# Attention and two gated layers on one core: the width in which ScalarE stores the scaled lower words of the weights

## The chip, the cores and the metric

The kernel runs on one core of one Trainium2 chip. The metric is the device time of one execution in microseconds (us), given as the median of several runs. Besides the time of each run there is one profiled execution of the kernel before, whose trace is quoted below.

## The reference

Windowed attention (4 batches, 8 heads, 576 positions, window of 64) feeds two gated layers in a row. Each layer multiplies 2304 tokens of width 512 with two weight matrices of 512 x 1536, gates one product by a function of the other, and multiplies the result with a third matrix of 1536 x 512.

```python
scores = scale * np.matmul(q, k.transpose(0, 1, 3, 2))       # then masked, softmax
x = np.matmul(attn, v)                                       # -> (2304, 512)
g = x @ w_gate; silu = g * (1.0 / (1.0 + np.exp(-g)))
x = (silu * (x @ w_val)) @ w_out                             # layer 1
...
gate = 1.0 / (1.0 + np.exp(-(x @ w_gate)))
out = (gate * (x @ w_val)) @ w_out                           # layer 2
```

Every one of the six weight matrices arrives as 64-bit floating point numbers, so it has to be turned into 32-bit numbers on the chip before TensorE can use it.

## The kernel before, in words

The tokens are cut into five tiles of 512, 384, 512, 512 and 384 tokens. For each layer and each tile the kernel walks over 12 slices of the hidden width; a slice has three steps: the product with the gate weights (tile `g`, function `product`), the product with the value weights (`v`), and one slice later the product with the output weights (`a`, function `out_product`). Each product is done as three matmul passes over numbers split into a high and a low part: `split_hi` on ScalarE writes the high part of a weight, `split_lo` on VectorE subtracts it. The order of the work on every engine is written out by hand: the string `START` gives the order of the first stretch (attention of the first four blocks of 128 tokens, and the first six weight conversions), and dictionaries of steps (`before`, `during`, `after`) attach all other work to a step of the products. Each engine takes its instructions in that order.

The conversion of one 128x512 piece of weights is in `round_a` and `round_b`. There are 72 such pieces, 36 for each layer. A piece lands in a tile `raw` with two 32-bit words for each number, a lower and an upper one, so the words of one kind stand 8 bytes apart. In `round_a`, ScalarE does two instructions: line 377 reads the lower words as unsigned integers, scales them so that only their top three bits remain as a number, and stores it; line 380 reads the upper words, takes the absolute value and writes it contiguously into a tile `t`. In `round_b`, VectorE does four: line 388 reads the top 16 bits of the upper word (`fourth`), keeps the sign, sets one more bit and stores that into the top half of the lower word (`second`); line 389 limits `t`, line 390 shifts it left by three, and line 391 adds the lower word to it, the sum being the 32-bit number. `conv_b` and `raw_ahead` then issue the next load of a `raw` tile, of which there are four. The converted output weights of layer 1 and all weights of layer 2 are also written to memory, to be loaded again for later tiles.

The conversions of layer 1 run before and during the first token tile of layer 1, those of layer 2 during its third and fourth. In the first stretch, `x_hi` (line 328) on ScalarE and `x_lo` (line 331) on VectorE bring a block's attention result into the tile `x`, which the products read; `evacuate` (line 211) brings transposed queries out for the scores, `evacuate_p` (line 308) transposed probabilities for the product with the values (`pv`, line 318).

Of the kernel before, what the change touches and what calls it, by code (L numbers as in the profile page):

```python
# [11 lines left out]
UINT32 = mybir.dt.uint32  # L12
UINT16 = mybir.dt.uint16
ACTF = mybir.ActivationFunctionType
# [25 lines left out]
def attention_moe_moe(  # L40
# [28 lines left out]
    scale = 1.0 / float(D) ** 0.5  # L69
# [269 lines left out]
    raws = {}  # L339
# [22 lines left out]
    def words_of(r):  # L362
        w = r.rearrange("p (f two) -> p f two", two=2)
        half = r.bitcast(UINT16).rearrange("p (f four) -> p f four", four=4)
        return w[:, :, 0], w[:, :, 1], half[:, :, 0], half[:, :, 1], half[:, :, 3]

# [3 lines left out]
    def round_a(key):  # L372
        t = t_p.tile([128, 512], INT32, tag="t", name="t")
        mids[key] = t
        if wide:
            lower, upper, first, _, _ = words_of(raws[key])
            nc.scalar.activation(  # L377
                out=first, in_=lower.bitcast(UINT32), func=ACTF.Copy, scale=2.0 ** -29
            )
            nc.scalar.activation(out=t.bitcast(FP32), in_=upper.bitcast(FP32), func=ACTF.Abs)  # L380

    def round_b(key, keep):
        r = raws.pop(key)
        t = mids[key]
        tf = t.bitcast(FP32)
        if wide:
            lower, _, _, second, fourth = words_of(r)
            nc.vector.tensor_scalar(second, fourth, 0x8000, 0x4000, ALU.bitwise_and, ALU.bitwise_or)  # L388
            nc.vector.tensor_scalar(tf, tf, F64_LEAST, F64_MOST, ALU.max, ALU.min)  # L389
            nc.vector.tensor_scalar(t, t, 3, None, ALU.logical_shift_left)  # L390
            nc.vector.tensor_tensor(out=t, in0=t, in1=lower, op=ALU.add)  # L391
        else:
            nc.vector.tensor_copy(tf, r)
        mids[key] = tf
        if keep:
            d = dram.tile([128, 512], FP32, name=f"k{key[0]}{key[1]}{key[2]}")
            nc.sync.dma_start(out=d, in_=tf)
            kept[key] = d
# [117 lines left out]
    for b in range(B):  # L516
# [4 lines left out]
        first = {1: 12, 2: 24, 3: 46}[b]  # L521
# [29 lines left out]
    def conv_b(j):  # L551
        round_b(convs[j][1], convs[j][1][1] == "o")
        raw_ahead(j + 1 + 4)

    for j, (s, key) in enumerate(convs[SPLIT_EARLY:], SPLIT_EARLY):
        at(during, s + 1, round_a, key)
        at(during, s + 2, round_b, key, key[0] == 1 or key[1] == "o")
        at(during, s + 2, raw_ahead, j + 1 + 4)
        if key[0] == 0:
            plan_split(s + 2, key)  # L560
# [32 lines left out]
    for t in range(NTL, 2 * NTL):  # L593
        for fc in range(FC):
            n, key = SPT * t + 3 * fc + 5, (1, "o", fc)
# [29 lines left out]
    with tc.manual_schedule():  # L625
# [13 lines left out]
        for step in LOADS.split():  # L639
# [31 lines left out]
            "lo": lambda i: x_lo(i, x_of(0), i * 128),  # L671
            "wm": lambda k: warm(k),
            "ca": lambda j: round_a(convs[j][1]),
            "cb": lambda j: conv_b(j),
            "ch": lambda j: split_hi(convs[j][1]),
# [9 lines left out]
        for T in range(2 * NTL):  # L685
# [3 lines left out]
            for fc in range(FC):  # L689
# [7 lines left out]
                    out=s, in_=gps[:, 0:n], func=(ACTF.Silu, ACTF.Sigmoid)[m]  # L697
# [54 lines left out]
```

## Time and profile before

| | |
|---|---|
| median of 3 runs | 1010.43 us (1010.13 to 1010.93) |
| profiled execution, its own time | 1010.98 us |
| span in its trace | 1009.2 us |
| TensorE matmul busy (PE) | 984.6 us, 98% of the span |
| VectorE busy (DVE) | 516.4 us, 51% |
| ScalarE busy (ACT) | 496.7 us, 49% |
| line 377, all 72 instructions | 98.0 us |

The span is the time from the first to the last instruction in the trace; 1.78 us of the profiled execution lie around it. PE, DVE, ACT and SP stand for TensorE, VectorE, ScalarE and the engine that issues most of the DMAs. Shares of busy time are averages over the whole span, while the stretches of the kernel differ: ScalarE and VectorE are nearly full in the first 155 us and mostly idle after 500 us.

### The profile page before, as it was taken

Reading aid. Unit: us, or ns where it says so; the run is one execution under the profiler, and the core shown is the slowest. Engines: PE = TensorE matmul, PEld = TensorE weight load, DVE = VectorE, ACT = ScalarE, POOL = GpSimd, SP = SyncE. Lnnn points to the kernel's source line nnn. Section 1 sums busy time; section 2 is a strip of 40 time slices with the busy share of each in tenths; the row PEclk is TensorE's granted clock in tenths of the full one; section 3 lists DMA queues with packets and bytes.
Section 4 is the critical chain, followed back from the end, with each engine's and each line's share of the span. In section 5 each row is a group of like instructions: output and inputs, shape, how many; then the busy total and the mean of one; then the engine's idle time right before and its main releaser. Section 6 shows DMA issues by size and latency. Waiting matters only on the chain.

```text
span 1009.2 us, 14684 instructions
## 1 busy us (share of the span) xinstructions
PE 984.6 (98%) x5621; PEld 847.7 (84%) x5621; DVE 516.4 (51%) x1181; ACT 496.7 (49%) x981; POOL 4.1 (0%) x20
## 2 busy tenths in 40 slices
PE   8899998999999999999999999999999999999998
PEld 6677777999878788888999888899988888888997
DVE  6899994554576777767555323223322222223322
ACT  6899994655676668657444322222222222222222
POOL 1000000000000000000000000000000000000000
PEclk7799999999999999999999999999999999999999
DMA  9647798773176666573644400020020002000100
GB/s 225 187 152 214 205 234 205 196 151 108 55 223 204 203 201 223 172 233 106 210 146 146 167 1 1 1 84 1 1 73 1 1 1 73 0 1 1 42 1 32
DMA packets 164982, 113.03 MB, mean 112 GB/s; under 512 B 102704, under 2 KB 139568, under 8 KB 164912
## 3 DMA queue, kind: packets, MB, share of 16 engines
q1 hardware_dynamic: 161264, 111.18, 38.1%
q10 hardware_dynamic: 3648, 0.92, 0.4%
q8 instruction: 44, 0.72, 0.3%
q14 instruction: 26, 0.21, 0.1%
HBM read 90.05 MB, written 27.53 MB: 117 GB/s over the span
## 4 chain that ended last, share of the span: by engine, by line
PE 80%; DVE 7%; ACT 7%; issue 3%; SPq 2%; DMA 1%; DVEq 0%; ACTq 0%
PE a L441 26%; PE g L429 26%; PE v L429 24%; ACT raw L377 2%; SPq L118 2%; ACT z L279 1%; DVE raw L388 1%; PE att L244 1%; PE att L318 1%; DVE t L390 1%; PE att L302 1%; DMA ks<-in_k_dram 1%; ACT L279 1%; DVE t L389 1%; DVE s L705 1%
## 5 line engine op out<-in xcount | busy, mean ns | idle before, releaser
L429 PE MATMUL g<-x,wg 128*128 128x512 f32 (+1 forms) x1440 | 319.5, 370 | 0.7 <-ACT x L328 0.7
L429 PE MATMUL v<-x,wv 128*128 128x512 f32 (+1 forms) x1440 | 317.6, 369 | 0.0
L429 PEld LDWEIGHTS g<-x,wg 128*128 128x128 f32 x1440 | 264.6, 189 | 38.0 <-ACT x L328 0.9
L429 PEld LDWEIGHTS v<-x,wv 128*128 128x128 f32 x1440 | 261.2, 188 | 33.0
L705 DVE TENSOR_TENSOR s<-s,v 128x512 f32<-128x512 f32 (+1 forms) x120 | 75.9, 632 | 314.7 <-PE v L429 303.6
L696 ACT ACTIVATE s<-g 128x512 f32<-128x512 f32 (+1 forms) x120 | 66.7, 556 | 304.1 <-PE g L429 303.6
L441 PE MATMUL a<-h,wo 128*128 128x512 f32 (+1 forms) x720 | 164.8, 377 | 6.3 <-DVE h L621 6.3
L441 PE MATMUL a<-wo,h 128*128 128x512 f32 x648 | 157.4, 390 | 0.0
L707 ACT ACTIVATE h<-s 128x512 fp32r<-128x512 f32 (+1 forms) x120 | 70.6, 588 | 169.4 <-DVE s L705 169.3
L441 PEld LDWEIGHTS a<-h,wo 128*128 128x128 f32 x720 | 131.2, 190 | 26.5 <-DVE h L621 7.6
L441 PEld LDWEIGHTS a<-wo,h 128*128 128x128 f32 x648 | 121.3, 188 | 24.2
L377 ACT ACTIVATE raw<-raw 128x512 uint16<-128x512 uint32 x72 | 98.0, 1361 | 0.0
L621 DVE TENSOR_TENSOR h<-s,h 128x512 fp32r<-128x512 f32 (+1 forms) x120 | 76.2, 635 | 3.2
L388 DVE TENSOR_SCALAR raw<-raw 128x512 uint16<-128x512 uint16 x72 | 53.9, 748 | 17.4 <-ACT raw L377 17.3
L279 ACT ACTIVATE z<-z,nm 128x128 f32<-128x128 f32 x144 | 55.8, 390 | 2.8 <-DVE nm L263 2.7
L101 DVE TENSOR_TENSOR x<-rx,x 128x512 fp32r<-128x512 f32 (+1 forms) x20 | 12.8, 639 | 84.3 <-ACT x L100 84.3
L391 DVE CUSTOM_DVE_ANT_0 t<-raw,t 128x1024 uint16<-128x1024 uint16 x72 | 49.9, 693 | 2.5
L380 ACT ACTIVATE t<-raw 128x512 f32<-128x512 f32 x72 | 51.1, 710 | 0.0
L415 DVE TENSOR_TENSOR wo<-stay,wo 128x512 fp32r<-128x512 f32 x60 | 41.1, 685 | 0.0
L411 ACT ACTIVATE wo<-stay 128x512 fp32r<-128x512 f32 x60 | 37.4, 623 | 0.0
L415 DVE TENSOR_TENSOR wo<-tw,wo 128x512 fp32r<-128x512 f32 x48 | 32.9, 686 | 5.7 <-ACT wo L411 5.7
L389 DVE TENSOR_SCALAR t<-t 128x512 f32<-128x512 f32 x72 | 33.3, 462 | 0.0
(84 smaller groups left out, 569.4 us busy)
## 6 DMA issues: line engine op xcount, KB each, us to landing
raw<-in_moe_w_gate_dram SPq DMA_DIRECT2D x24, 512.0 KB, 4.2
raw<-in_moe_w_val_dram SPq DMA_DIRECT2D x24, 512.0 KB, 4.3
raw<-in_moe_w_out_dram SPq DMA_DIRECT2D x24, 512.0 KB, 3.7
tw<-k0o SPq DMA_DIRECT2D x48, 256.0 KB, 4.2
v<-in_v_dram SPq DMA_DIRECT2D x29, 256.0 KB, 4.6
out_dram<-o SPq DMA_DIRECT2D x18, 256.0 KB, 2.3
k<-ks SPq DMA_DIRECT2D x10, 384.0 KB, 5.4
k0o<-t SPq DMA_DIRECT2D x12, 256.0 KB, 2.3
```

Of the source, the lines that this page charges most:

```text
L279: nc.scalar.activation(out=z[:, hp, :], in_=z[:, hp, :], func=ACTF.Exp, scale=-1.0, bias=nm[:, hp:hp + 1], accum_out=su[:, hp:hp + 1],)
L377: nc.scalar.activation(out=first, in_=lower.bitcast(UINT32), func=ACTF.Copy, scale=2.0 ** -29)
L380: nc.scalar.activation(out=t.bitcast(FP32), in_=upper.bitcast(FP32), func=ACTF.Abs)
L388: nc.vector.tensor_scalar(second, fourth, 0x8000, 0x4000, ALU.bitwise_and, ALU.bitwise_or)
L391: nc.vector.tensor_tensor(out=t, in0=t, in1=lower, op=ALU.add)
L415: nc.vector.tensor_tensor(out=w[:, 1], in0=mids.pop(key), in1=w[:, 0].bitcast(FP32), op=ALU.subtract)
L429: nc.tensor.matmul(out=ps[:, 0:n], lhsT=w[:, a, c, :], rhs=xt[:, b, c, 0:n], start=(j == 0), stop=(j == len(mm) - 1),)
L441: nc.tensor.matmul(out=acc[e][:, 0:n] if m == 0 else acc[e], lhsT=w[:, a, cols] if m == 0 else h[:, a, cols], rhs=h[:, b, 0:n] if m == 0 e ...
L621: nc.vector.tensor_tensor(out=h[:, 1, 0:n], in0=s, in1=h[:, 0, 0:n].bitcast(FP32), op=ALU.subtract)
L696: nc.scalar.activation(out=s, in_=gps[:, 0:n], func=(ACTF.Silu, ACTF.Sigmoid)[m])
L705: nc.vector.tensor_tensor(out=s, in0=s, in1=vps[:, 0:n], op=ALU.mult)
L707: nc.scalar.activation(out=h[:, 0, 0:n], in_=s, func=ACTF.Copy)
```

## The change

The store of line 377 goes to the whole lower word as a 32-bit integer, where it went to the lower half of that word as a 16-bit integer. The upper half, which was left alone before, is now written too; VectorE's line 388 overwrites it afterwards as it did before. No instruction is added, removed or moved on any engine or DMA queue, and no instruction waits for another kind of event than before.

```diff
     def words_of(r):
         w = r.rearrange("p (f two) -> p f two", two=2)
         half = r.bitcast(UINT16).rearrange("p (f four) -> p f four", four=4)
-        return w[:, :, 0], w[:, :, 1], half[:, :, 0], half[:, :, 1], half[:, :, 3]
+        return w[:, :, 0], w[:, :, 1], half[:, :, 1], half[:, :, 3]
...
         if wide:
-            lower, upper, first, _, _ = words_of(raws[key])
+            lower, upper, _, _ = words_of(raws[key])
             nc.scalar.activation(
-                out=first, in_=lower.bitcast(UINT32), func=ACTF.Copy, scale=2.0 ** -29
+                out=lower, in_=lower.bitcast(UINT32), func=ACTF.Copy, scale=2.0 ** -29
             )
...
         if wide:
-            lower, _, _, second, fourth = words_of(r)
+            lower, _, second, fourth = words_of(r)
```

## Rows read from the trace of the kernel before

**Rows 1.** The page, part 1: busy time, share and instructions of each engine.
```profile
PE 984.6 (98%) x5621; PEld 847.7 (84%) x5621; DVE 516.4 (51%) x1181; ACT 496.7 (49%) x981; POOL 4.1 (0%) x20
```

**Rows 2.** Busy time by stretch: length, PE, PEld, DVE, ACT, POOL; clock, DMA, GB/s.
```profile
8.00:43.50 35.50, 29.00 (x307) 23.32 (x303) 30.00 (x118) 31.93 (x95) 0.00 (x0) 0.66 0.88 210
...
51.80:155.00 103.20, 93.47 (x550) 74.38 (x546) 99.58 (x232) 97.30 (x173) 0.00 (x0) 0.98 0.74 206
...
200.00:500.00 300.00, 298.25 (x1939) 254.16 (x1938) 198.24 (x490) 194.78 (x392) 0.00 (x0) 1.00 0.58 175
```

**Rows 3.** Groups of ScalarE's instructions by line and shape (busy us, mean ns).
```profile
L377 ACT ACTIVATE raw<-raw 128x512 uint16<-128x512 uint32 x72 | 98.0, 1361 | 0.0
...
L380 ACT ACTIVATE t<-raw 128x512 f32<-128x512 f32 x72 | 51.1, 710 | 0.0
...
L411 ACT ACTIVATE wg<-t 128x512 fp32r<-128x512 f32 x12 | 7.5, 623 | 1.8 <-DVE t L391 1.8
```

**Rows 4.** Timeline of 36 to 44 us: start, duration, instruction, [idle before <-releaser].
```profile
35.62 1.36 ACT L377 ACTIVATE raw<-raw 128x512 uint16<-128x512 uint32 x1
...
36.70 0.73 ACT L380 ACTIVATE t<-raw 128x512 f32<-128x512 f32 x1
...
37.33 0.59 ACT L308 ACTIVATE pt<-a 128x512 f32<-128x512 f32 x1
...
37.80 1.34 ACT L377 ACTIVATE raw<-raw 128x512 uint16<-128x512 uint32 x1
...
39.48 0.59 ACT L328 ACTIVATE x<-a 128x512 fp32r<-128x512 f32 x1
...
40.10 0.69 DVE L331 TENSOR_TENSOR x<-a,x 128x512 fp32r<-128x512 f32 x1 [0.68 <-ACT x L328]
...
40.71 0.75 DVE L388 TENSOR_SCALAR raw<-raw 128x512 uint16<-128x512 uint16 x1
...
40.85 1.98 PE L318 MATMUL a<-pt,v 128*64 128x64 f32 x32 [2.75 <-DVE x L331]
...
41.24 0.47 DVE L389 TENSOR_SCALAR t<-t 128x512 f32<-128x512 f32 x1
...
43.52 0.80 PE L429 MATMUL g<-x,wg 128*128 128x512 f32 x1 [0.70 <-ACT x L328]
```

**Rows 5.** Timeline of 20.4 to 29 us.
```profile
21.88 1.35 ACT L377 ACTIVATE raw<-raw 128x512 uint16<-128x512 uint32 x1
...
24.07 1.36 ACT L377 ACTIVATE raw<-raw 128x512 uint16<-128x512 uint32 x1
...
26.41 1.33 PE L244 MATMUL v<-kt,early_q 64*64 64x128 f32 x10 [0.66 <-ACT early_q L211]
```

**Rows 6.** All waits of VectorE, 50 to 156 us (us in total, times, longest).
```profile
DVE s L705 <- PE v L429: 2.5, 1, 2.5
DVE x L331 <- ACT x L328: 1.2, 2, 0.6
```

**Rows 7.** Waits of TensorE from 156 us to the end.
```profile
PE att L302 <- DVE z L294: 0.9, 2, 0.6
...
PE att L244 <- DVE kt L231: 0.8, 2, 0.5
```

**Rows 8.** Waits of VectorE, 260 to 484 us.
```profile
DVE raw L388 <- ACT raw L377: 15.5, 12, 1.8
```

**Rows 9.** Waits of TensorE, 8 to 156 us.
```profile
PE a L441 <- DVE h L621: 6.3, 3, 2.1
```

**Rows 10.** Stretches around the first products, columns as in Rows 2.
```profile
40.00:41.00 1.00, 0.15 (x2) 0.15 (x4) 0.90 (x2) 1.00 (x4) 0.00 (x0) 0.51 0.28 98
...
46.00:47.00 1.00, 1.00 (x5) 0.77 (x4) 1.00 (x3) 0.66 (x2) 0.00 (x0) 0.58 0.91 309
```

**Rows 11.** Stretches after two of the waits of Rows 9, same columns.
```profile
113.00:114.00 1.00, 1.00 (x5) 0.82 (x5) 1.00 (x3) 1.00 (x3) 0.00 (x0) 1.00 0.90 291
...
156.00:157.00 1.00, 1.00 (x4) 0.77 (x4) 0.78 (x2) 0.79 (x2) 0.00 (x0) 0.53 0.80 209
```

## The prediction, made before the changed kernel ran

> **What bounds the kernel now.** I read the table of engines first: TensorE is busy for 98% of the span [rows 1], so an engine that gets faster elsewhere can only give back what TensorE loses by waiting. The stretches say where that is. From 200 to 500 us TensorE is busy for 298.25 of 300 us, although half of all conversions lie there. From 8 to 43.5 us and from 51.8 to 155 us it is idle for 6.5 and 9.7 us [rows 2]. In the second of these the reader is to see two nearly full engines: VectorE busy for 99.58 of 103.20 us, ScalarE for 97.30. The waits say which of the two is the bound. In 106 us VectorE waits three times in all, 3.7 us, and once the first tile's work has begun only twice for 0.6 us each, both in line 331 for line 328 [rows 6]. TensorE meanwhile waits three times for VectorE's low half of the hidden values, 6.3 us [rows 9]. So the first tile runs at VectorE's pace, with ScalarE close behind; before it the small pieces of the start follow each other from engine to engine; after it TensorE sets the pace. The time of line 377, 98 us in 72 instructions [rows 3], must not be read as time to be gained.
>
> **The price of the new store.** Line 377 takes 1361 ns. Its neighbour, line 380, reads words 8 bytes apart of the same tile and writes them contiguously in 710 ns, and a contiguous copy of the same size takes 623 ns [rows 3]. So reading every second word costs some 90 ns, and about 650 ns of line 377 must come from its 16-bit store with gaps, from the integer formats or from working in place. No row has a 32-bit store with gaps. The timeline shows more than the mean: after line 377 starts at 35.62, line 380 starts at 36.70, 1.08 us later, while line 377 is recorded until 36.98, so 0.28 us overlap. Line 380 holds the engine for 0.63 us and overlaps its follower by 0.10 us [rows 4]. When the next instruction starts to read, line 377 still has a longer backlog to write than others. That speaks for the store, rather than for reading or converting, as the slow end. Against it: VectorE's line 388 also stores 16 bits every 8 bytes and lets its follower start after 0.53 us [rows 4], so such a store is not slow on every engine. The bounds for a 32-bit store with gaps are the contiguous copy, 623 ns, and the row of line 377 itself, 1361 ns; twice its excess over the copy is the far end of the slower rival below. I take 710 ns, since the other side of the same tile, in the same 8-byte steps and whole words, is the nearest row. That frees 0.65 us of latency and 1.08 - 0.63 = 0.45 us of ScalarE's time for each conversion, 32 us in all 72.
>
> A rule speaks against that. The rows show 1361 ns for 2-byte stores in 8-byte steps and 710 ns for 4-byte reads in the same steps [rows 3]. The Trainium skill, page "SBUF — State Buffer", section "Specifications (TRN2)", has lines of 16 bytes and wants two hits in a line for full bandwidth. By that rule both stores hit each line twice, the width would change nothing, and the sum would be zero; no row before shows whether it holds for ScalarE's stores, and the 1361 ns sit badly with it. What it would give is the second rival.
>
> **What of it reaches the end.** No instruction moves, and the wait of line 388 for line 377 stays. So the change is a shorter instruction, and what counts is where ScalarE is waited for.
>
> At the start, six conversions lie before the first product. Two stand ahead of the copy of queries that the scores at 26.41 wait for, at 21.88 and 24.07; TensorE is idle for 0.66 us there [rows 5]. Two savings of 0.45 us are more than that, so the gain is 0.66 us. Two more stand at 35.62 and 37.80, ahead of line 328 at 39.48; line 331 waits for it for 0.68 us, TensorE waits for line 331 until 40.85, and the first product starts at 43.52 behind that [rows 4]. Two savings again exceed the 0.68 us, after which VectorE's own work is the limit. Together 0.66 + 0.68 = 1.3 us.
>
> In the first tile 28 conversions give ScalarE 28 x 0.45 = 12.6 us of room, but VectorE has only its two waits, 1.2 us, to give up [rows 6]. This is the cover that makes the rest worth nothing: VectorE's own 99.6 us of work [rows 2], of which the change touches none. If VectorE did not bind, TensorE's 9.7 idle us would be the limit. What is late next is VectorE.
>
> Later, 36 conversions run behind a full TensorE. VectorE waits 15.5 us for line 377 there [rows 8], but TensorE's own waits after 156 us that these can feed are 0.9 us for line 294 and 0.8 us for line 231 [rows 7], two each. Line 377 ending 0.65 us earlier removes a wait as long as the larger, if it stands behind it on VectorE; I count half, 0.8 us.
>
> The sum is 1.3 + 1.2 + 0.8 = 3.3 us off a profiled execution of 1010.98 us (span 1009.2 and 1.78 around it), 1007.7 us; that execution was 0.55 us above the median of 1010.43, so the median goes to **1007.1 us**.
>
> **Rivals.**
> *The clock stays up at the start.* TensorE idles for 2.75 us before 40.85 and then runs at half clock, 0.51 in 40 to 41 and still 0.58 in 46 to 47 [rows 4, 10]. The idle stretch would shrink to about 2.1 us. The three later waits of 2.1 us [rows 9] went both ways: the clock was full after one and 0.53 after another [rows 11]. If it holds here, some 6 us at half clock become 3, and the time is 1007.1 - 3 = 1004 us.
>
> *The store's price stays.* For it: a 16-bit store on VectorE that keeps pace, and integer formats that stay the same. Against it: the backlog. Then nothing moves: 1010.4 us.
>
> *The price falls half-way*, to about 1.03 us. The 0.23 us saved for each conversion give 0.46 at each place of the start, 0.9 in all, about 1.0 in the first tile and 0.5 later: 1008.0 us.
>
> *The price falls and the clock takes it back.* If a wait of TensorE such as that at 113 to 114 is met with half clock near 155 us, where TensorE takes over the pace, 3 us at half clock cost 1.5 us: 1008.6 us. Earlier in the first tile VectorE's pace would cover it.
>
> *Slower:* the price goes with the bytes stored. The excess over the contiguous copy, 1361 - 623 = 738 ns, would double. ScalarE's idle time in the first tile is 103.2 - 97.3 = 5.9 us [rows 2], 0.21 us for each of 28 conversions; from that increase on ScalarE is the bound in place of VectorE. At 0.74 us it is 28 x 0.74 - 5.9 = 14.8 us there and 4 x 0.74 = 3 us at the start: 1028 us. Nothing in the rows speaks for it but that whole words are twice the bytes, and line 380, which reads as many in the same steps quickly, speaks against.
>
> **How the numbers follow.** Chances: my forecast 0.45, with a range of its own of 1005 to 1009 us (none of the later waits but all of the start and the tile, or the start half only, up; all 1.7 us of the later waits and some clock, down); the clock stays up 0.08; half-way 0.10; price unchanged 0.25; taken back by the clock 0.06; slower 0.06. About 0.2%, 2.0 us, is what a measurement of this kernel can tell from no change, so faster means below 1008.4 us. That holds for most of the forecast, for the kept clock and for a part of the half-way case: 0.54. Unchanged price, the give-back and the rest of these make 0.37 for the same; slower 0.09. The range, 1003.8 to 1011.2 us, takes in the kept clock and the unchanged price with their scatter, and leaves out the slower rival and rarer sums of good luck.
>
> **What the changed profile would show.** If the price step is right, line 377 has a mean near 710 ns and the next instruction starts about 0.6 us after it, with an overlap of 0.1 us. If the start is right, the first product begins near 42.2 us, with no wait of line 331 near 39 us. If the bound is right, VectorE stays 99 to 100 us busy in the first tile while ScalarE gains some 13 us of idle time, most of it waiting for line 705, and TensorE goes on waiting for line 621. If the later step is right, TensorE's waits for lines 231 and 294 after 156 us shrink, and VectorE's wait of 15.5 us for line 377 halves. The prediction is wrong if the mean of line 377 stays above 1.2 us, if VectorE's instructions change in length, since its pace carries the first tile, or if the granted clock falls in other places than before.

## The result, and the profile after

The changed kernel takes 1001.19 us in the median of four runs (1000.38 to 1004.74), against 1010.28 us before. The ratio is 0.9916 with a 95% interval of 0.9891 to 0.9942. Measured again with more runs of the kernel before beside it, it took 1001.23 us, ratio 0.9898 (0.9884 to 0.9913). So the gain is 9 to 10 us, where 3.3 us were forecast, and the time lies below the stated range.

The page of the changed kernel, part 1, shows ScalarE with some 40 us less work and the other engines as they were [rows 1].

```profile
PE 980.4 (98%) x5621; PEld 844.7 (84%) x5621; DVE 515.6 (52%) x1181; ACT 457.0 (46%) x981; POOL 4.1 (0%) x20
```

The groups of ScalarE's instructions by shape (busy us, mean ns) show where it went. Line 377 fell from 1361 to 666 ns [rows 3].

```profile
L380 ACT ACTIVATE t<-raw 128x512 f32<-128x512 f32 x72 | 47.9, 666 | 0.0
L377 ACT ACTIVATE raw<-raw 128x512 int32<-128x512 uint32 x72 | 47.9, 666 | 0.0
```

The timeline of the last part of the start, in the changed kernel, answers to [rows 4]. The second instruction now follows 0.57 us after line 377 starts, and the overlap is 0.14 us. Line 331 no longer waits for line 328; TensorE waits for it for 1.32 us in place of 2.75, and runs the product of line 318 in 1.15 us in place of 1.98.

```profile
35.85 0.71 ACT L377 ACTIVATE raw<-raw 128x512 int32<-128x512 uint32 x1
...
36.42 0.69 ACT L380 ACTIVATE t<-raw 128x512 f32<-128x512 f32 x1
...
36.99 0.61 ACT L328 ACTIVATE x<-a 128x512 fp32r<-128x512 f32 x1
...
38.06 0.68 DVE L331 TENSOR_TENSOR x<-a,x 128x512 fp32r<-128x512 f32 x1
...
38.80 1.15 PE L318 MATMUL a<-pt,v 128*64 128x64 f32 x32 [1.32 <-DVE x L331]
...
40.65 0.74 PE L429 MATMUL g<-x,wg 128*128 128x512 f32 x2 [0.70 <-ACT x L328]
```

The same stretches as in [rows 10] have the full clock now (the column behind POOL).

```profile
40.00:41.00 1.00, 0.35 (x2) 0.31 (x3) 0.97 (x3) 1.00 (x2) 0.00 (x0) 1.00 0.88 360
46.00:47.00 1.00, 1.00 (x6) 0.75 (x4) 0.55 (x1) 1.00 (x4) 0.00 (x0) 1.00 0.88 273
```

In the first tile ScalarE is busy for 78.02 of 94.10 us, VectorE for 91.88.

```profile
47.40:141.50 94.10, 89.50 (x525) 71.95 (x526) 91.88 (x217) 78.02 (x166) 0.00 (x0) 0.96 0.74 205
```

Of TensorE's waits after 156 us, one is left, which the kernel before has too; the two of [rows 7] are gone.

```profile
PE att L202 <- DVE x L331: 0.8, 1, 0.8
```

To see where the time came from, I compare the start of a few instructions in the two traces. The columns are the first product, then the 1st, 10th, 13th, 25th and 48th of the 120 instructions of line 705 (VectorE's product of gate and value), and the span. The first row has the times of the kernel before; the others show how much earlier (-) or later (+) each kernel's one profiled execution is. Rows with a name in e are the experiments below.

```
                   product   1st    10th    13th    25th    48th     span
before               43.52  51.79  146.25  176.53  266.81  480.74  1009.18
after                -2.88  -4.37   -5.82   -6.04   -6.09   -8.98    -8.98
e5_after_again       -3.34  -3.00   -4.49   -4.78   -4.82   -7.77    -7.62
e2_start_only        -4.49  -6.03   -5.14   -5.16   -5.20   -5.13    -5.13
e3_tile_only         -1.11  -0.78   -2.19   -0.92   -0.63   -0.55    -0.55
e4_layer2_only       -1.45  -0.14   +0.35   -0.93   -0.62   -3.52    -3.51
e6_before_warm       -1.56  -3.10   -2.31   -2.35   -2.04   -2.03    -2.03
e7_after_h_first     -3.18  -4.71   -6.17   -7.20   -7.19  -10.08   -10.07
e8_before_no389      +0.29  +0.43   -2.61   -3.31   -2.99   -2.96    -2.96
e10_after_no389      -4.93  -6.46  -18.81  -15.67  -14.73  -17.61   -17.60
```

In the changed kernel three stretches gain: 4.4 us up to line 705's first instruction, 1.4 us in the first tile (1st to 10th), and 2.9 us between the 25th and the 48th, where the second layer's weights are converted. The forecast had 1.3, 1.2 and 0.8 us.

### The profile page after: what moved, and what is told of

It is laid out like the page before. It is cut to its first block, busy times and chain, and to the rows that moved or that the text cites. A ratio compares the mean times of both kernels' runs of the same rounds, so it can differ in the third digit from the quotient of the medians.

```text
span 1000.2 us, 14684 instructions
## 1 busy us (share of the span) xinstructions
PE 980.4 (98%) x5621; PEld 844.7 (84%) x5621; DVE 515.6 (52%) x1181; ACT 457.0 (46%) x981; POOL 4.1 (0%) x20
## 4 chain that ended last, share of the span: by engine, by line
PE 86%; DVE 9%; issue 2%; DMA 1%; ACT 1%; SPq 0%; DVEq 0%
PE a L441 28%; PE g L429 27%; PE v L429 27%; DVE raw L388 2%; PE att L318 1%; DVE t L390 1%; PE att L244 1%; PE att L302 1%; DVE t L391 1%; DVE t L389 1%; DVE z L263 1%; DVE h L621 1%; DVE s L705 1%; DMA raw<-in_moe_w_val_dram 1%; DVE wv L415 0%
## 5 line engine op out<-in xcount | busy, mean ns | idle before, releaser
L391 DVE CUSTOM_DVE_ANT_0 t<-raw,t 128x1024 uint16<-128x1024 uint16 x72 | 49.8, 692 | 2.5
L380 ACT ACTIVATE t<-raw 128x512 f32<-128x512 f32 x72 | 47.9, 666 | 0.0
L377 ACT ACTIVATE raw<-raw 128x512 int32<-128x512 uint32 x72 | 47.9, 666 | 0.0
```

Of the source, the lines that this page charges most:

```text
L377: nc.scalar.activation(out=lower, in_=lower.bitcast(UINT32), func=ACTF.Copy, scale=2.0 ** -29)
```

## The experiments

### What makes the store slow

In the first kernel the second layer's 36 pieces store the scaled words in eight forms by turns, each on a line of its own (here in words):

```diff
-    nc.scalar.activation(out=lower, in_=word, func=Copy, scale=2.0 ** -29)
+    L383: out = 16-bit integers every 8 bytes in raw     L385: out = lower (32-bit integers every 8 bytes)
+    L387: out = 512 packed 16-bit integers in t          L389: out = 16-bit integers every 4 bytes in t
+    L391: out = bf16 every 8 bytes in raw                L393: out = lower as 32-bit floats
+    L395: out = 256 16-bit integers every 8 bytes in t   L397: out = 32-bit integers, packed, in t
```

> The first layer's pieces are converted as in the changed kernel; the 36 pieces of the second layer store the scaled lower words in eight forms by turns, of which only two give the right weights. Theory (half of a 32-bit word is the slow thing): 16-bit integers every 8 bytes near 1.36 us, bf16 every 8 bytes the same, 16-bit integers every 4 bytes over 1 us, half as many 16-bit integers every 8 bytes into another tile near 0.78 us; 32-bit integers and 32-bit floats every 8 bytes 0.67 us; packed 16-bit integers and packed 32-bit integers near 0.62 us. Rival A (the integer formats): bf16 every 8 bytes takes 0.67 us. Rival B (working in place): 16-bit integers into another tile run at 0.62 us for 512 and 0.42 us for 256. Rival C (gaps of any kind): the 16-bit form every 4 bytes is faster than that every 8 bytes, and 32-bit stores with gaps are slower than packed ones by as much.

The groups by shape, with the mean in ns behind the busy time:

```profile
L385 ACT ACTIVATE raw<-raw 128x512 int32<-128x512 uint32 x40 | 26.8, 670 | 0.0
...
L391 ACT ACTIVATE raw<-raw 128x512 bf16<-128x512 uint32 x5 | 6.8, 1354 | 0.0
L383 ACT ACTIVATE raw<-raw 128x512 uint16<-128x512 uint32 x4 | 5.4, 1360 | 0.0
...
L395 ACT ACTIVATE t<-raw 128x256 uint16<-128x256 uint32 x5 | 3.9, 771 | 0.0
L393 ACT ACTIVATE raw<-raw 128x512 f32<-128x512 uint32 x5 | 3.3, 662 | 0.0
L397 ACT ACTIVATE t<-raw 128x512 int32<-128x512 uint32 x5 | 3.3, 655 | 0.3 <-DVE wo L433 0.3
...
L389 ACT ACTIVATE t<-raw 128x512 uint16<-128x512 uint32 x4 | 3.1, 783 | 0.0
L387 ACT ACTIVATE t<-raw 128x512 uint16<-128x512 uint32 x4 | 2.6, 650 | 0.0
```

A bf16 store is as slow as one of 16-bit integers, so the integer formats are not it (rival A falls). A store into another tile is as slow for each element, so working in place is not it (rival B falls). Gaps alone are not it either: 32-bit words every 8 bytes take 670 ns, packed ones 655. Half words are slow only where they leave gaps, and there I missed: every 4 bytes they take 783 ns, not over 1 us. So 512 of them over 2 KB cost as much as 256 over 2 KB. A second kernel of the same kind separates the two ways to read that, called theory A and theory B in its expectation, with stores in 16- and 32-byte steps, 256 packed half words (L391) and single bytes every 8 bytes (L393):

```diff
+    L385: 256 16-bit integers every 16 bytes    L387: 128 16-bit integers every 32 bytes
+    L389: 256 32-bit integers every 16 bytes    L395: 128 32-bit integers every 32 bytes
+    L391: 256 16-bit integers, packed           L393: 512 8-bit integers every 8 bytes
```

> The second layer's 36 pieces are converted in six forms by turns that treat only a part of the words, or store bytes, so their weights are not the right ones; the first layer is as in the changed kernel. The forms before gave 1.36 us for 512 half words every 8 bytes, 0.78 for 512 every 4 bytes and 0.77 for 256 every 8 bytes, so the price followed the length that the store spans. Theory A (each 8-byte piece that is written in part costs 2.3 ns): 256 half words every 16 bytes take 0.78 us, 128 every 32 bytes 0.48 us, 512 bytes every 8 bytes 1.36 us. Theory B (each 16-byte piece costs 4.6 ns): 256 half words every 16 bytes take 1.36 us, 128 every 32 bytes 0.78 us. Both: 32-bit words every 16 and 32 bytes stay near the time of a contiguous store of as many, 0.4 and 0.3 us, or pay for their reads; 256 packed half words 0.4 us.

```profile
L393 ACT ACTIVATE raw<-raw 128x512 uint8<-128x512 uint32 x6 | 8.2, 1361 | 0.0
L385 ACT ACTIVATE raw<-raw 128x256 uint16<-128x256 uint32 x6 | 8.1, 1358 | 0.0
...
L387 ACT ACTIVATE raw<-raw 128x128 uint16<-128x128 uint32 x6 | 4.6, 764 | 0.0
L389 ACT ACTIVATE raw<-raw 128x256 int32<-128x256 uint32 x6 | 4.0, 662 | 0.0
...
L395 ACT ACTIVATE raw<-raw 128x128 int32<-128x128 uint32 x6 | 2.7, 454 | 0.0
L391 ACT ACTIVATE t<-raw 128x256 uint16<-128x256 uint32 x6 | 2.5, 422 | 0.0
```

Theory B holds. A store of half words with gaps touches 256 pieces of 16 bytes in the first and 128 in the second of each pair (512 every 8 and every 4 bytes; 256 every 16 and 128 every 32 bytes), and costs (1360 - 783) / 128 = 4.5 ns and (1358 - 764) / 128 = 4.6 ns for each piece, however many half words fall into it. 32-bit words in the same places cost less: 670 for 1360 ns, 662 for 1358, 454 for 764. They are not free of gaps either: 256 of them every 16 bytes take as long as 512 every 8 bytes, and longer than the 0.4 us that I expected of a contiguous store. Whether their reads or their stores pay that is not shown.

### Which conversions give the time

Three kernels use the new store for a part of the 72 conversions and the old one for the rest (`conv_at` has a piece's place in the list of conversions):

```diff
-                out=first, in_=lower.bitcast(UINT32), func=ACTF.Copy, scale=2.0 ** -29
+                out=lower if conv_at[key] < SPLIT_EARLY else first, ...            # start_only
+                out=lower if SPLIT_EARLY <= conv_at[key] < 3 * FC else first, ...  # tile_only
+                out=lower if conv_at[key] >= 3 * FC else first, ...                # layer2_only
```

> Only the first six conversions store 32-bit words. Theory (the start gains 1.3 us by shorter waits and about 3 us more because TensorE's clock stays up through the first products): 4.4 us faster than before, 1005.9 us, first product near 40.7 us. Rival (the first tile is where ScalarE is the bound): under 1.5 us faster.

Measured: 1006.95 us, ratio 0.9971 (0.9963 to 0.9980) beside 1010.5 us before: 3.5 us. The start is the largest part, a little smaller than expected. The twelve runs spread from 1005.85 to 1009.88 us, and the profiled one is the fastest of them, so the table shows a better case than the median. In it the start gains 6.0 us, and 0.9 of them are lost in the first tile, where ScalarE still has its long stores. VectorE waits for it there as in [rows 6], and once more for line 377:

```profile
DVE x L331 <- ACT x L328: 1.2, 2, 0.6
...
DVE raw L388 <- ACT raw L377: 0.6, 1, 0.6
```

> Only the 30 conversions of the first layer that run after the first product store 32-bit words. Theory (VectorE sets the pace of the first tile and gains only its two waits of 0.6 us): 1.2 to 1.5 us faster, 1008.9 us. Rival (ScalarE is the bound of the first tile): 5 us faster or more.

Measured: 1010.06 us, ratio 0.9991 (0.9983 to 1.0000). That is 0.4 us, less than expected and at the edge of the noise. Within the tile the trace gains 1.4 us (-0.78 to -2.19), as the theory had it, and gives 1.3 back at its end, where TensorE's clock is at half for longer: the granted clock from 152 to 159 us is 0.52, and 0.79 in the kernel before. The rival with 5 us falls.

> Only the 36 conversions of the second layer store 32-bit words. Theory (TensorE's matmul waits of 1.7 us go, and its waits of 0.3 us for weights of the attention's last product, which stand behind ScalarE, go too): 2.9 us faster, 1007.4 us. Rival (my forecast, half of the matmul waits alone): 0.8 us faster, 1009.5 us.

Measured: 1007.65 us, ratio 0.9974 (0.9964 to 0.9985). The trace gains 2.9 us between the 25th and the 48th line 705, as the changed kernel does, and nothing is gained there in the two kernels above. My forecast of 0.8 us falls. The matmuls' waits of 1.7 us are gone, as the theory had it, but its second half has the wrong mechanism. It took the gaps of 0.35 us ahead of the weight loads of line 318 for lost time. Seven such gaps, 2.5 us, stand between 260 and 484 us in the kernel before:

```profile
PEld att L318 <- ACT h L707: 1.1, 3, 0.4
...
PEld att L318 <- issue: 0.7, 2, 0.4
PEld att L318 <- ACT t L380: 0.7, 2, 0.4
```

Over the same work the changed kernel has seven again, 2.5 us. Only what they are put down to differs ("issue" is a gap in which the engine waited for nothing that the profile shows):

```profile
PEld att L318 <- issue: 2.1, 6, 0.4
...
PEld att L318 <- ACT pt L308: 0.4, 1, 0.4
```

What goes is inside the products. In the kernel before, three of the seven products of line 318, at 335.3, 428.8 and 465.3 us, take 1.47 to 1.48 us; the other four take 1.15, and so do all seven here and in the changed kernel. The timelines of one of the three, before (427.5 to 430.3 us) and in the changed kernel (416 to 422.5 us), show the cause. The product starts before line 308 has written the second half of the probabilities (until 429.06), and cannot end before it has them; in the changed kernel line 308 is done first (at 420.05):

```profile
427.23 0.68 DVE L705 TENSOR_TENSOR s<-s,v 128x512 f32<-128x512 f32 x1
...
428.48 0.58 ACT L308 ACTIVATE pt<-att 128x512 f32<-128x512 f32 x1
...
428.79 1.47 PE L318 MATMUL att<-pt,v 128*64 128x64 f32 x32
```

```profile
418.22 0.68 DVE L705 TENSOR_TENSOR s<-s,v 128x512 f32<-128x512 f32 x1
...
419.47 0.58 ACT L308 ACTIVATE pt<-att 128x512 f32<-128x512 f32 x1
...
420.46 1.15 PE L318 MATMUL att<-pt,v 128*64 128x64 f32 x32
```

Line 308 follows line 705 by 1.25 us in both; but line 705 starts 1.56 us ahead of the product before and 2.24 us ahead of it after. So it is VectorE that was behind, and it waited for line 377 for 15.5 us in this part [rows 8], 7.8 us in the changed kernel. The 1.7 us of matmul waits and 3 x 0.33 = 1.0 us inside the products make 2.7 of the 2.9 us. The theory's 2.9 us came out by luck: the gaps that it counted are still there, and time that it did not know of went in their place.

### The whole again

> The changed kernel once more, for a closer figure. Theory (the parts add: about 3.4 us at the start, 0.7 us in the first tile, 2.7 us later): 6 to 9 us faster than before. Rival (the parts help each other beyond their sum): 9 us or more.

Measured: 1001.23 us beside 1010.4 us, 9.2 us between the medians; the ratio, 0.9898 (0.9884 to 0.9913), would make it 10.3. The three parts alone give 3.5 + 0.4 + 2.9 = 6.8 us between medians, so the rival is nearer: they help each other. What the traces show of that is the 0.9 us which a faster start loses in the first tile when ScalarE has its old stores there (0.8 in e6 below). The other 1.5 us are within what the intervals of four kernels, some 1 us each, can hide, and stay open; the 1.3 us that the kernel with the tile alone gives back at the tile's end may be a part of them.

### TensorE's clock at the first products

The kernel before with eight idle matmuls more, ahead of the product with the values of the fourth block, and no other store:

```diff
-... pv2 hi2 po3 wo3 lo2 ...
+... pv2 hi2 po3 wm8 wo3 lo2 ...
```

> The kernel before, with eight idle matmuls more in TensorE's wait of 2.75 us ahead of the fourth block's product with the values; no store is changed. Theory (a part of the gain at the start is TensorE's clock, which falls in that wait): the clock stays full there in most executions, the first product group takes 3.1 us instead of 4.6, and the kernel is 1 to 2 us faster. Rival (the start gains only by ScalarE's shorter line): no difference, 1010.5 us.

Measured: 1009.55 us, ratio 0.9992 (0.9984 to 1.0001). The 0.9 us between the medians are not clear of the noise, and less than expected. The profiled execution is the fastest of the eleven. In its trace the product with the values takes 1.15 us after a wait of 0.86 us:

```profile
36.55 2.09 PE L634 MATMUL warm<-idle 128*128 128x512 f32 x8
39.50 1.15 PE L318 MATMUL a<-pt,v 128*64 128x64 f32 x32 [0.86 <-DVE x L331]
```

The first line 705 starts 3.1 us earlier, of which 0.8 are lost in the tile, as with the kernel that only has the faster start. Put beside the other traces, with TensorE's wait ahead of that product and the clock in the products behind it, this tells the parts of the start's gain apart:

```
store in the start   idle matmuls   kernel: wait us -> clock, start of the first line 705
16-bit               no             before 2.75 -> half, 51.79;  e3 2.12 -> half, 51.01
                                    e4 2.81 -> half, 51.66;  e8 2.96 -> half, 52.22
16-bit               yes            e6 0.86 -> full, 48.70
32-bit               no             e1 1.99 -> half, 49.01;  e5 1.98 -> half, 48.80;  e9 1.91 -> half, 50.52
                                    after 1.32 -> full, 47.42;  e2 1.29 -> full, 45.77
                                    e7 1.30 -> full, 47.09;  e10 1.04 -> full, 45.33
32-bit               yes            e11 1.08 -> full, 47.40;  e12 0.36 -> full, 45.85
```

Without idle matmuls the mean is 51.7 us with the 16-bit store; with the 32-bit store and half clock it is 49.4, with full clock 46.4. So the shorter store goes with 2.2 us, and the clock that stays up, as it did in four of these seven executions, with another 3.0 us.

Not all of the 3.0 us is the clock's. Executions of one start differ ahead of that product too: the granted clock from 8 to 36 us lies between 0.63 and 0.88 with the 16-bit store and between 0.70 and 0.94 with the 32-bit one. Counted from the start of the product to the first line 705, full clock gives 8.6 us in all four and half clock 10.3 to 11.4, 2.4 us more in the mean; the rest of the 3.0 us lies ahead of the product.

In the one trace with idle matmuls and the 16-bit store, the same stretch takes 9.2 us where it takes 10.9 to 12.1 without them, 2.1 us less than the mean. Since the medians do not show a gain of this size, what the clock at this place is worth end to end stays open.

### Who is the bound in the first tile

Line 389 is left out in the 30 conversions that run in the first tile, once with the old store and once with the new one:

```diff
-            nc.vector.tensor_scalar(tf, tf, F64_LEAST, F64_MOST, ALU.max, ALU.min)
+            if not SPLIT_EARLY <= conv_at[key] < 3 * FC:
+                nc.vector.tensor_scalar(tf, tf, F64_LEAST, F64_MOST, ALU.max, ALU.min)
```

> The kernel before without the limiting of line 389 in the 30 conversions of the first tile, so that part of the computation is left out; VectorE gets 30 x 0.5 = 15 us less work there, ScalarE none. Theory (VectorE sets the pace of the first tile, ScalarE stands close behind with 5.9 us of idle time): 3 to 6 us faster, with ScalarE full. Rival (ScalarE is already the bound): no difference.

Measured: 1008.6 us, ratio 0.9979 (0.9971 to 0.9988), 1.8 us between the medians, less than expected; the tile itself gains 3.0 us in the trace, the lower end of what was expected. ScalarE is then the fuller engine, 88.00 of 93.00 us:

```profile
52.00:145.00 93.00, 86.24 (x515) 69.17 (x515) 82.06 (x190) 88.00 (x158) 0.00 (x0) 0.98 0.74 201
```

> The changed kernel without the limiting of line 389 in the 30 conversions of the first tile, so that part of the computation is left out: 15 us less work for VectorE there. Theory (VectorE is the bound of the first tile, and after the change ScalarE no longer stands close behind it): the first tile shrinks by 6 us or more, twice what the same cut gave in the kernel before, until TensorE is full; 994 to 996 us. Rival (both engines bind alike, or transfers do): 3 us as in the kernel before, 998 us.

Measured: 994.38 us, ratio 0.9848 (0.9830 to 0.9866) beside 1009.96 us before. In the trace the tile is 12.4 us shorter than in the kernel before (-6.46 to -18.81), 10.9 us shorter than in the changed one, and TensorE is full in it:

```profile
45.30:128.50 83.20, 82.95 (x512) 67.33 (x513) 80.75 (x190) 74.87 (x159) 0.00 (x0) 1.00 0.81 221
```

Of this, 3.1 us are lost again by the 13th line 705, behind the tile. The same cut of VectorE's work, 15 us, is worth nearly four times as much once ScalarE is no longer close behind: 10.9 us for 3.0 in the tile, and 6.8 us (from the changed kernel's 1001.2) for 1.8 in the medians. VectorE was the bound in the tile before and after, but before it could have given up only 3 us before ScalarE took its place.

### Two attempts at more

VectorE's low half of the hidden values ahead of the conversions of its step:

```diff
-                at(during, g + 2, hidden_lo, h, s, n, first=False)
+                at(during, g + 2, hidden_lo, h, s, n, first=True)
```

> The changed kernel with VectorE's low half of the hidden values ahead of the conversions of its step instead of behind them. Theory (in the first tile VectorE is the bound and TensorE's three waits of 2.1 us for line 621, with the half clock that follows the last of them, are its queue): the waits go, and the kernel is 2 to 4 us faster than the changed one, 998 us. Rival (VectorE's total work alone sets the end of the tile): the waits move to the weights, within 1 us of the changed kernel.

Measured: 1000.76 us, ratio 0.9907 (0.9887 to 0.9927), no difference from the changed kernel. TensorE's three waits for line 621, 6.4 us, are gone, and other waits stand in their place:

```profile
PE att L202 <- DMA q<-in_q_dram: 3.5, 2, 1.9
PE att L318 <- ACT pt L308: 1.3, 1, 1.3
```

The tile takes as long as before this edit (-4.71 to -6.17, against -4.37 to -5.82): VectorE's work sets its end in either order, as the rival had it.

Four idle matmuls more at the place of e6, in the changed kernel (`wm4`), alone and with that order:

> The changed kernel with four idle matmuls more ahead of the fourth block's product with the values. Theory (TensorE's clock at the first products still falls in some executions of the changed kernel and costs 2 to 3 us when it does): a median 1 to 2 us below the changed kernel's 1001.2 us, about 999.8. Rival (it does not fall there after the change): no difference.

> The same with VectorE's low half of the hidden values ahead of the conversions of its step as well. Theory (with the early order TensorE has no fall of the clock where it takes over the pace near 150 us): 1 to 2 us below the version with four idle matmuls alone, about 998.5 us. Rival (VectorE's work sets the end of the tile in either order): the same as that version.

Measured: 1000.82 us, ratio 0.9904 (0.9889 to 0.9919), and 1001.24 us, ratio 0.9913 (0.9898 to 0.9928). Neither differs from the changed kernel, where 1 to 2 us less were expected at each step; the intervals, 1.5 us either way, could hide 1 us. The clock is full at the first products in both traces, but it was so in the changed kernel's own trace too, and the first kernel has the changed kernel's falls to half at 67, 108 and 149 us as well. No version with all of its work beats the changed kernel.

## Why the prediction was wrong

**The price of the new store** was right: 666 ns against 710 forecast, and the reason held, since the backlog of writes that the overlap of 0.28 us hinted at is the store's [rows 4]. ScalarE gains a little more than forecast, 39.7 us in 72 conversions or 0.55 us each in place of 0.45: line 380 now starts 0.51 us sooner behind line 377, and became shorter itself, 666 ns in place of 710. Three of the rivals (the price stays, it falls half-way, it goes with the bytes stored) fall with it. The rule of the Trainium skill, page "SBUF — State Buffer", section "Specifications (TRN2)", by which two hits in a line of 16 bytes are enough, does not hold for these stores: half words every 8 bytes hit each line twice and take 1360 ns, words in the same places 666. The length of 16 bytes agrees with what the two price kernels show.

**The start** is the step that failed most: 1.3 us forecast, 4.4 us in the profiled execution, 3.5 us in the median of the kernel that has the new store only there. Two terms were mis-sized.

The first is the clock, which was taken as given, so its term was nothing. "The clock stays up at the start" was a rival with a chance of 0.08 and a price of 3 us. In the traces it stays up in four of seven executions with the new store and in none of the four with the old one, and is worth some 2.4 us there. I expected TensorE's wait ahead of the product to shrink from 2.75 to 2.1 us; it was 2.1 to 3.0 us with the old store and came down to 1.0 to 2.0 us. What the engine did before a full clock was a wait of 0.4 to 1.3 us, and before a half clock one of 1.9 to 3.0 us, in all fourteen traces. That the wait decides it here is argued from these and from the one trace in which idle matmuls shorten the wait with the old store; the median of that kernel does not confirm the price. One of the forecast's own signs of being wrong, falls of the clock in other places than before, came true.

The second is the two waits themselves, 0.66 + 0.68 = 1.3 us, read from one execution. With the clock at half in both, the means differ by 2.2 us. The executions of the two groups spread by 1.2 and 1.7 us themselves (51.01 to 52.22 and 48.80 to 50.52), so this is no clear miss. A part of it can be seen at line 331: from the end of line 294 to the end of line 331, the stretch of VectorE that TensorE's wait covers, the kernel before takes 3.5 us and all five executions with the old store 3.5 to 4.2, 3.8 in the mean. With the new store it is 2.7 us in eight of nine (3.4 in e9). So the term of 0.68 us was right for the execution from which it was read, and about 1 us against the mean. The rest stays open.

**The first tile** was right: 1.4 us against 1.2, with VectorE at 91.88 of 94.10 us and both waits of line 331 gone. The step that VectorE binds holds on both sides of the change; ScalarE stands close behind it before the change only.

**The later waits** were mis-sized: 2.9 us against 0.8. I counted half of the matmuls' waits of 1.7 us, and all of them went. Time lost inside a product was put at nothing; there another 1.0 us went, where line 308 came too late for three products of line 318. The sign that VectorE's wait of 15.5 us for line 377 would halve came true (7.8 us). What failed is the step from there to TensorE: VectorE's delay reached it through lines 705 and 308 as well.

By these traces the sum should have been 2.2 + 1.4 + 2.9 = 6.5 us with the clock as it was, and 8.9 us with the clock up. The medians gained 9.1 and 9.2 us, although the clock was up in four of seven executions only, so the account does not close to the last microsecond.

## What to carry to other kernels

A store of half words with gaps is worth a look in any profile: compare its mean with that of a whole-word store of as many elements. An engine that is not the bound of a stretch can still be late for single instructions, and such a delay need not stand in any row of waits: it can be hidden in a product that starts before its last operand is there and takes 1.47 us in place of 1.15. A row of waits is lost time only if it goes with its cause; the gaps of 0.35 us ahead of the weight loads did not. And where two engines are both nearly full, an edit to either is worth little until the other has been relieved; the same cut of VectorE's work shortened the tile by 3 us before this change and by 11 us after it.

## What was not expected of the hardware

ScalarE's stores of 8- and 16-bit elements with gaps cost about 4.6 ns for each 16-byte piece that they touch: 1361 ns for 512 single bytes and 1360 for 512 half words every 8 bytes, 1358 for 256 half words every 16 bytes. Packed half words (650 ns) and whole words with the same gaps (666 ns) do not pay this. VectorE's line 388, which also stores 16 bits every 8 bytes, takes 750 ns, so VectorE does not pay that price.

Executions of one program differ by where TensorE's clock falls to half in the first 160 us: in the two traces of the changed kernel the granted clock from 8 to 36 us is 0.70 and 0.82, and at the first products it is full in one and half in the other. The changed kernel's runs spread over 999.3 to 1004.7 us, though nothing in the program differs; how much of that is the clock's is not shown, and what decides the clock beyond the waits named above stays open.
